# Gated attention on one core: where the output projection's sums of the first half are kept

## The chip, the core and the metric

The kernel runs on one core of a Trainium2 chip. Its engines work side by side, each through its own instructions in order: TensorE (PE in the profile, its weight loads PEld), VectorE (DVE), ScalarE (ACT), GpSimd (POOL) and SyncE (SP), which here only issues DMAs. GpSimd can issue DMAs too. The metric is the device time of one execution in microseconds (us).

## What is computed

One input x (2048 rows, 640 columns) is normalised row by row. From it come an attention over cached keys and values (32 heads of 128, the last 512 cached positions) with an output projection, and a gate from a two-layer network. Everything is float32.

```
xn = layernorm(x)
q  = xn @ wq                                  # per head: 2048 x 128
p  = softmax(q @ k.T * 128**-0.5)             # 512 cached positions
s  = sum over heads of (p @ v) @ wo[head]     # 2048 x 640
h  = relu(xn @ w1 + b1)**2
g  = silu(h @ w2 + b2)
out = x + s * g
```

The change concerns how the sum over heads in s is kept for the first half of the rows.

## The kernel before

**Products.** Each float32 factor is split into a high and a low part (tiles that end in 0 and 1 or hi and lo), and a product is three matmuls (`triple`). A column tile holds NT = 512 rows of x. There are four such tiles t; the first two are half 0 (hf = 0), the others half 1.

**Units.** The network of the gate runs first, for three of the four tiles. Then attention runs in 128 units. A unit is one head on one tile. In a half, heads go in 16 groups g of G = 2; a group runs tile 0 with both heads, then tile 1 with both heads: four units. A unit is spread over about three periods of PERIOD = 12.4 us of the plan, so that in each period TensorE works on parts of several units.

**The order.** Every step is put into a list with a time by `at` and `on`; the list is sorted by that time and each step is written out, so the time fixes only the order on each engine. `Ordered` keeps that order. Within a period, after the s matmuls (scores, in PSUM), VectorE folds the maxima (rdm), ScalarE gathers them, VectorE writes a row of them (rowm), SyncE sends it to DRAM (m_d) and reads it back broadcast to all partitions (bm, `row`). Then `shift` subtracts it on VectorE, e<-s,bm, which frees the s banks for the s matmuls of the next unit. ScalarE takes the exponential (e<-e) and the high part (pt_0_0, pt_1_0), and GpSimd the low parts (pt_0_1, pt_1_1) and the sum su. The o matmuls of the next period use pt. The raw weights come 10 us ahead of use and are split by ScalarE and GpSimd (wq, wk, wv, wo).

**The sums.** After the second head of a tile, `r_mm` multiplies both heads' outputs ot with wo, in five chunks d of 128 output columns, each into one PSUM bank r_d. `r_acc` empties it. In the first group (g = 0) ScalarE copies the bank into the tile acc (128 x 5 x 512); in the fifteen others VectorE adds the bank to acc in place. There are two acc tiles, one for each tile of the half (tag acc, bufs=TPH=2). After the last group of half 0, SyncE stores each chunk to s_d in DRAM (L591), ten stores of 256 KB, and the two tiles are taken over by half 1. `load_finish` and `finish` read s_d back later, during half 1, and form the output.

The five chunks are emptied at these places of the plan, counted from the start of the unit of the second head: d = 0 just past the start of the third period after it, d = 1 within that period, and d = 3, 2 and 4 in the fourth.

## Time and profile before

| | us |
|---|---|
| median of 3 runs | 1992.19 (1991.41 to 1992.53) |
| the profiled execution | 1990.35 |
| its span, first to last instruction | 1988.6 |
| plain part of the first half, 395 to 1034 | 49.2 per group of four units |
| additions acc<-r,acc on VectorE, both halves | 300, 662 ns each |
| copies acc<-r on ScalarE, first groups of both halves | 20, 577 ns each |
| stores s_d<-acc on SyncE's queue | 10, 256 KB each, 3.3 to landing |

A row of a timeline gives the start in us, the duration, the engine, the line (L72 is the helper that keeps the order, and so stands for nearly all of attention), the operation, out<-in, the count, and in brackets how long the engine had been idle and whom it waited for. A row of a window gives its length, each engine's busy time with its instructions, TensorE's granted clock, the busy share of the DMA engines and GB/s. A row of a group gives the count, the busy time in us, the mean in ns, and the idle time ahead.

### The profile page before, as it was taken

The page shows a single profiled execution, that of the slowest core. Times are in us where ns is not written, and L with a number is a line of the kernel's source. Part 1 is how long each engine was busy: PE and PEld are TensorE (multiplying, and loading weights), DVE is VectorE, ACT ScalarE, POOL GpSimd, SP SyncE. Part 2 cuts the span into 40 slices and gives each one's busy share as a digit, 9 for nine tenths or more (in the row PEclk, how much of TensorE's full clock was granted, in tenths as well). Part 3 has the DMA queues.
Part 4 walks back from the last instruction along what each step waited for, and adds up shares of the span by engine and source line. Part 5 has one row for each costly group of instructions (what it writes and reads, how often), then busy time and mean ns, then how long its engine had stood idle before and what let it go on. Part 6 is the DMA issues. An engine that isn't in the chain of part 4 may idle for free.

```text
span 1988.6 us, 25917 instructions
## 1 busy us (share of the span) xinstructions
PE 1958.7 (98%) x8576; PEld 1603.1 (81%) x8576; DVE 1515.5 (76%) x2511; ACT 1186.3 (60%) x2034; POOL 1375.3 (69%) x755
## 2 busy tenths in 40 slices
PE   7999999999999999999999999999999999999998
PEld 6788887788888888888887788888888888888877
DVE  5523236788888888888888878888888888888864
ACT  4432326766666666666666676666666666666643
POOL 1121225888888888888887788888888888888841
PEclk9999999999999999999999999999999999999999
DMA  4421444322323233222335433333333333333354
GB/s 137 136 106 38 180 171 144 105 91 94 95 93 91 91 91 91 91 90 92 94 93 170 157 98 107 112 112 113 112 112 115 113 112 113 96 91 91 110 147 141
DMA packets 126871, 220.39 MB, mean 111 GB/s; under 512 B 21542, under 2 KB 36304, under 8 KB 125456
## 3 DMA queue, kind: packets, MB, share of 16 engines
q1 hardware_dynamic: 123744, 204.28, 32.9%
q0 software_dynamic: 2992, 14.43, 1.8%
q8 instruction: 69, 1.13, 0.2%
q14 instruction: 66, 0.54, 0.1%
HBM read 194.26 MB, written 24.39 MB: 110 GB/s over the span
## 4 chain that ended last, share of the span: by engine, by line
PE 88%; DMA 4%; DVE 4%; ACT 2%; issue 1%; POOL 1%; SPq 0%; POOLq 0%; DVEq 0%; ACTq 0%
PE pq L72 20%; PE r L72 20%; PE o L72 17%; PE s L72 17%; PE py L96 2%; PE py L97 2%; PE py L95 2%; PE ph L97 2%; PE ph L96 2%; PE ph L95 2%; PE ly L72 2%; PE lu L72 1%; DMA w1r<-in_w_dram 1%; DMA bm<-m_d 1%; DVE rdm L72 1%
## 5 line engine op out<-in xcount | busy, mean ns | idle before, releaser
L72 POOL TENSOR_TENSOR pt<-e,pt 128x1024 fp32r<-128x1024 f32 x256 | 616.2, 2407 | 120.4 <-ACT pt L72 120.4
L72 PE MATMUL r<-ot,wo 128*128 128x512 f32 x1920 | 496.9, 389 | 0.2 <-DVE acc L72 0.2
L72 PE MATMUL pq<-ax,wq 128*128 128x512 f32 x1920 | 456.6, 389 | 0.8 <-DMA ax<-xT_d 0.7
L72 PEld LDWEIGHTS pq<-ax,wq 128*128 128x128 f32 x1920 | 360.6, 188 | 76.3 <-DMA ax<-xT_d 1.5
L72 PEld LDWEIGHTS r<-ot,wo 128*128 128x128 f32 x1920 | 360.3, 188 | 75.6 <-DVE acc L72 0.6
L72 PE MATMUL s<-q,wk 128*128 128x512 f32 x1536 | 372.1, 391 | 5.9 <-DVE e L72 5.9
L72 PE MATMUL o<-pt,wv 128*128 128x512 f32 x1536 | 374.6, 392 | 1.4 <-DVE ot L72 1.2
L72 ACT ACTIVATE e<-e 128x1024 f32<-128x1024 f32 x256 | 269.9, 1054 | 126.0 <-DVE e L72 122.1
L72 PEld LDWEIGHTS s<-q,wk 128*128 128x128 f32 x1536 | 287.9, 188 | 70.7 <-issue 7.2
L72 PEld LDWEIGHTS o<-pt,wv 128*128 128x128 f32 x1536 | 283.5, 188 | 72.9 <-DVE ot L72 14.9
L72 DVE TRANSPOSE_TENSOR_REDUCE rdm<-s 128x16 f32<-128x512 f32 (+1 forms) x384 | 313.4, 868 | 36.9 <-PE s L72 36.2
L72 DVE TENSOR_TENSOR e<-s,bm 128x512 f32<-128x512 f32 (+1 forms) x384 | 304.3, 842 | 17.0 <-DMA bm<-m_d 16.8
L72 POOL TENSOR_TENSOR su<-e,e 128x1024 f32<-128x1024 f32 x128 | 307.6, 2403 | 0.0
L72 ACT ACTIVATE pt<-e 128x1024 fp32r<-128x1024 f32 x256 | 272.0, 1062 | 7.9
L237 POOL TENSOR_TENSOR r<-r 128x512 f32<-128x512 f32 (+1 forms) x42 | 44.1, 1051 | 227.9 <-ACT r L278 208.8
L72 DVE TENSOR_TENSOR acc<-r,acc 128x512 f32<-128x512 f32 x300 | 198.6, 662 | 2.7 <-PE r L72 2.7
L72 ACT ACTIVATE ot<-o 128x512 fp32r<-128x512 f32 x128 | 76.8, 600 | 197.1 <-DVE o L72 197.1
L72 ACT ACTIVATE rds<-rds 32x32 f32<-32x32 f32 x384 | 87.7, 228 | 128.5 <-DVE rds L72 125.5
L72 DVE TRANSPOSE_TENSOR_REDUCE rds<-su 128x32 f32<-128x1024 f32 x128 | 158.1, 1235 | 0.1
L72 DVE TENSOR_TENSOR ot<-o,ot 128x512 fp32r<-128x512 f32 x128 | 88.6, 692 | 85.2 <-ACT ot L72 85.2
L72 POOL TENSOR_TENSOR wv<-vr,wv 128x512 fp32r<-128x512 f32 x64 | 83.2, 1300 | 81.5 <-ACT wv L72 74.4
L72 POOL TENSOR_TENSOR wq<-qr,wq 128x640 fp32r<-128x640 f32 x62 | 97.7, 1576 | 60.2 <-ACT wq L72 60.2
(123 smaller groups left out, 2168.6 us busy)
## 6 DMA issues: line engine op xcount, KB each, us to landing
bm<-m_d SPq DMA_DIRECT2D x128, 256.0 KB, 3.2
bs<-s_d SPq DMA_DIRECT2D x128, 256.0 KB, 3.8
qr<-in_wq_dram SPq DMA_DIRECT2D x64, 320.0 KB, 4.1
or<-in_wo_dram SPq DMA_DIRECT2D x64, 320.0 KB, 4.1
kr<-in_kT_dram SPq DMA_DIRECT2D x64, 256.0 KB, 3.4
vr<-in_v_dram SPq DMA_DIRECT2D x64, 256.0 KB, 4.3
xT_d<-xT POOLq DMA_DIRECT2D x6, 1280.0 KB, 7.5
xb<-in_x_dram SPq DMA_DIRECT2D x16, 320.0 KB, 3.4
```

The source lines that it names most:

```text
L72: ins = method(*args, **kwargs)
L95: nc.tensor.matmul(ps, ah, bh, start=first and i == 0, stop=False)
L96: nc.tensor.matmul(ps, ah, bl, start=False, stop=False)
L97: nc.tensor.matmul(ps, al, bh, start=False, stop=last and i == n - 1)
L237: nc.gpsimd.tensor_tensor(r, r, r, op=ALU.mult)
```

## The change

In half 0 every group is now treated like the first: ScalarE copies each bank into an acc tile, which is a new one for each tile and group (the same two buffers in turn). After the fifth chunk, a new step `r_store` sends the whole tile, 1280 KB, to s_d from GpSimd's queue with one DMA. In group 0 that DMA writes; in the others it adds to what is in DRAM (accum_op), with the five chunks of a partition as five pieces. SyncE's ten stores are gone. Half 1 is as before.

```diff
     def r_acc(i, d):
         hf, g, t, h = units[i]
         pr = PRS.pop((i, d))
+        if d == 0 and (hf == 0 or g == 0):
+            ACC[hf, t] = keep.tile(
+                [P, DC, NT], F32, tag="acc", name=f"acc{hf}_{t}_{g}", bufs=TPH
+            )
+        a = ACC[hf, t][:, d, :]
+        if hf == 0 or g == 0:
+            act.activation(a, pr, AF.Copy)
+        else:
+            dve.tensor_tensor(a, pr, a, op=ALU.add)
+
+    def r_store(i):
+        hf, g, t, h = units[i]
         if g == 0:
-            if d == 0:
-                ACC[hf, t] = keep.tile(
-                    [P, DC, NT], F32, tag="acc", name=f"acc{hf}_{t}", bufs=TPH
-                )
-            act.activation(ACC[hf, t][:, d, :], pr, AF.Copy)
+            pool.dma_start(s_d[t], ACC[hf, t])
         else:
-            a = ACC[hf, t][:, d, :]
-            dve.tensor_tensor(a, pr, a, op=ALU.add)
-        if g == NG - 1 and hf == 0:
-            sp.dma_start(s_d[t][:, d, :], ACC[hf, t][:, d, :])
+            pool.dma_start(s_d[t], ACC[hf, t], accum_op=ALU.add, max_dma_last_dim=4 * NT)
...
                     on(when + 0.68 * len(js), r_acc, i, d)
+                if d == DC - 1 and hf == 0:
+                    on(4 * PERIOD + 9.2, r_store, i)
```

ScalarE's order in one odd period of the second group, before (e is the exponential, rdm the gather of maxima, rds that of sums, ot and q high parts, wv and wq weights):

```order
L72 ACTIVATE e_0_3440<-e_0_3440 128x1024 [waits DVE_49,Pool_49]
L72 ACTIVATE pt_0_0_3465<-e_0_3440 128x1024 [waits Activation_49]
L72 ACTIVATE e_1_3449<-e_1_3449 128x1024 [waits DVE_49,Pool_49]
L72 ACTIVATE pt_1_0_3484<-e_1_3449 128x1024 [waits PE_49,Activation_49]
L72 ACTIVATE rdm_3476<-rdm_3476 32x64 [waits DVE_49]
L72 ACTIVATE rdm_3476<-rdm_3476 32x64 x2
L72 ACTIVATE ot_3515<-o_3426 128x512 [waits DVE_49]
L72 ACTIVATE q_0_3527<-pq_3495 128x512 [waits PE_49]
L72 ACTIVATE rds_3524<-rds_3524 32x32 [waits DVE_49]
L72 ACTIVATE rds_3524<-rds_3524 32x32 x2
L72 ACTIVATE wv_5_0_3542<-vr_5_3442 128x512 [waits DMAHW0_49]
L72 ACTIVATE wq_6_0_3546<-qr_6_3444 128x640 [waits DMAHW1_49]
```

The same place now:

```order
L72 ACTIVATE acc_0_1_3338<-r_3_3454 128x512 [waits PE_49]
L72 ACTIVATE pt_0_0_3468<-e_0_3443 128x1024 [waits Activation_49]
L72 ACTIVATE e_1_3452<-e_1_3452 128x1024 [waits DVE_49,Pool_49]
L72 ACTIVATE pt_1_0_3487<-e_1_3452 128x1024 [waits Activation_49]
L72 ACTIVATE rdm_3479<-rdm_3479 32x64 [waits DVE_49]
L72 ACTIVATE rdm_3479<-rdm_3479 32x64 x2
L72 ACTIVATE acc_0_1_3338<-r_2_3406 128x512 [waits PE_49]
L72 ACTIVATE ot_3518<-o_3429 128x512 [waits DVE_49]
L72 ACTIVATE q_0_3530<-pq_3498 128x512 [waits PE_49]
L72 ACTIVATE rds_3527<-rds_3527 32x32 [waits DVE_49]
L72 ACTIVATE rds_3527<-rds_3527 32x32 x2
L72 ACTIVATE acc_0_1_3338<-r_4_3533 128x512 [waits PE_49]
```

Three copies have come in: ahead of pt_0_0, ahead of ot, and behind rds, where the weight splits wv and wq follow as before. In an even period there are two, of r_0 ahead of pt_0_0 and of r_1 ahead of ot. The copy of r_0 is the first into its tile and waits for the store that last read that buffer:

```order
L72 ACTIVATE acc_1_1_3596<-r_0_3583 128x512 [waits DMASW4_49,PE_49]
L72 ACTIVATE pt_0_0_3598<-e_0_3572 128x1024 [waits Activation_49]
L72 ACTIVATE e_1_3581<-e_1_3581 128x1024 [waits DVE_49,Pool_49]
L72 ACTIVATE pt_1_0_3617<-e_1_3581 128x1024 [waits Activation_49]
L72 ACTIVATE rdm_3609<-rdm_3609 32x64 [waits DVE_49]
```

These rows follow two weight splits behind the ones above, in the next even period, and belong to tile 1. DMASW is a count that a DMA of GpSimd's queue raises when it has landed.

GpSimd's order at the end of the same odd period and in the even one behind it, before (su is the sum of e):

```order
L72 TENSOR_TENSOR wv_5_1_3543<-vr_5_3442,wv_5_0_3542 128x512 [waits DMAHW0_49,PE_49,Activation_49]
L72 TENSOR_TENSOR wq_6_1_3547<-qr_6_3444,wq_6_0_3546 128x640 [waits DMAHW1_49,Activation_49]
L72 TENSOR_TENSOR pt_0_1_3594<-e_0_3568,pt_0_0_3593 128x1024 [waits Activation_49,Pool_49]
L72 TENSOR_TENSOR su_3626<-e_0_3568,e_1_3577 128x1024 [waits Activation_49]
L72 TENSOR_TENSOR pt_1_1_3613<-e_1_3577,pt_1_0_3612 128x1024 [waits Activation_49]
```

And now:

```order
L72 TENSOR_TENSOR wv_5_1_3546<-vr_5_3445,wv_5_0_3545 128x512 [waits DMAHW0_49,PE_49,Activation_49]
L72 TENSOR_TENSOR wq_6_1_3550<-qr_6_3447,wq_6_0_3549 128x640 [waits DMAHW1_49,Activation_49]
L72 DMA s_d_77<-acc_0_1_3338 128x5x512 [waits DMASW5_49,DMASW3_49]
L72 TENSOR_TENSOR pt_0_1_3599<-e_0_3572,pt_0_0_3598 128x1024 [waits Activation_49,Pool_49]
L72 TENSOR_TENSOR su_3631<-e_0_3572,e_1_3581 128x1024 [waits Activation_49]
L72 TENSOR_TENSOR pt_1_1_3618<-e_1_3581,pt_1_0_3617 128x1024 [waits PE_49,Activation_49]
```

The store has come in between the weight splits and the three long instructions on e. It waits for the store before it into the same sum.

## The prediction

> **What bounds the kernel now.** I read the busy times first, then a table of stages by windows, then one pair of periods of the first half instruction by instruction. A period starts with the s matmuls of one unit. Even periods hold the sums of r_0 and r_1 of a group, odd ones those of r_3, r_2 and r_4.

> ```profile
> PE 1958.7 (98%) x8576; PEld 1603.1 (81%) x8576; DVE 1515.5 (76%) x2511; ACT 1186.3 (60%) x2034; POOL 1375.3 (69%) x755
> core 0: us, PE busy (x) PEld busy (x) DVE busy (x) ACT busy (x) POOL busy (x), PEclk, DMA share, GB/s
> 641.00:690.20 49.20, 49.20 (x219) 40.49 (x218) 42.15 (x71) 32.33 (x57) 39.96 (x21) 1.00 0.29 92
> ...
> 1034.60:1084.00 49.40, 48.61 (x213) 39.41 (x212) 41.24 (x70) 31.82 (x56) 38.80 (x21) 1.00 0.50 155
> 1084.00:1133.00 49.00, 47.07 (x206) 37.92 (x204) 39.79 (x66) 30.26 (x51) 38.83 (x20) 1.00 0.49 162
> 1133.00:1182.00 49.00, 48.57 (x214) 39.91 (x213) 38.05 (x64) 34.75 (x63) 38.92 (x21) 1.00 0.35 113
> ```

> TensorE is busy in all 49.20 us of a group of four units, at full clock. Work taken from VectorE there has no gap of TensorE to fill. The only losses near the change lie at the turn between the halves: 0.79, 1.93 and 0.43 us, 3.15 in all. So the question is not what the change frees but which of TensorE's just-in-time inputs it makes late. Two matter: the row of maxima that goes out to DRAM and comes back broadcast (m_d, then bm) before VectorE can subtract it and free the s bank, and GpSimd's low parts pt before the o matmuls.

> ```profile
> 659.07 0.32 SPq L72 DMA_DIRECT2D m_d<-rowm  x1
> 659.96 2.41 POOL L72 TENSOR_TENSOR pt<-e,pt 128x1024 fp32r<-128x1024 f32 x1
> 660.42 0.33 SPq L72 DMA_DIRECT2D bm<-m_d  x1
> 661.70 2.93 PE L72 MATMUL o<-pt,wv 128*128 128x512 f32 x12
> 664.22 2.37 DVE L72 TENSOR_TENSOR e<-s,bm 128x1024 f32<-128x1024 f32 x3
> 665.83 2.88 PE L72 MATMUL s<-q,wk 128*128 128x512 f32 x12
> ...
> 671.36 0.33 SPq L72 DMA_DIRECT2D m_d<-rowm  x1
> 676.22 2.37 DVE L72 TENSOR_TENSOR e<-s,bm 128x1024 f32<-128x1024 f32 x3
> 677.15 1.59 POOL L72 TENSOR_TENSOR wq<-qr,wq 128x640 fp32r<-128x640 f32 x1
> 678.07 2.88 PE L72 MATMUL s<-q,wk 128*128 128x512 f32 x12
> 679.78 2.41 POOL L72 TENSOR_TENSOR pt<-e,pt 128x1024 fp32r<-128x1024 f32 x1 [1.04 <-ACT pt L72]
> ```
> ```profile
> bm<-m_d SPq DMA_DIRECT2D x128, 256.0 KB, 3.2
> L72 DVE TENSOR_TENSOR e<-s,bm 128x1024 f32<-128x1024 f32 x128 | 151.3, 1182 | 17.0 <-DMA bm<-m_d 16.8
> ```

> In the even period bm is issued at 660.42 and lands 3.2 us later, at 663.6. The next s matmuls start at 665.83 and need the first subtraction, 1.18 us, so it may start at 664.65: **bm has 1.0 us to spare**. The odd period has less, as a late one shows:

> ```profile
> 695.90 0.33 SPq L72 DMA_DIRECT2D m_d<-rowm  x1
> 698.14 0.33 SPq L72 DMA_DIRECT2D bm<-m_d  x1
> 701.46 2.42 DVE L72 TENSOR_TENSOR e<-s,bm 128x1024 f32<-128x1024 f32 x3 [0.64 <-DMA bm<-m_d]
> 702.83 1.39 PE L72 MATMUL s<-q,wk 128*128 128x512 f32 x5
> ```

> Here m_d took 2.24 us where it mostly takes 1.35 (660.42 less 659.07). VectorE waited 0.64, the subtraction ended at 702.64, and the s matmuls at 702.83 just held.

> **The change, part by part.** Removed are 150 additions on VectorE, added 150 copies on ScalarE:

> ```profile
> L72 DVE TENSOR_TENSOR acc<-r,acc 128x512 f32<-128x512 f32 x300 | 198.6, 662 | 2.7 <-PE r L72 2.7
> L72 ACT ACTIVATE acc<-r 128x512 f32<-128x512 f32 x20 | 11.5, 577 | 0.0
> ```

> VectorE loses 150 x 0.662 = 99 us of work. That is worth nothing, since TensorE is full and covers it. ScalarE gains 150 x 0.577 = 87 us; per group 32.3 + 10 x 0.577 = 38.1 of 49.2, which fits. What counts is what a copy delays behind it in ScalarE's order. One stands between e and pt in every period. The first group of the half already has its copies on ScalarE, so this is in the trace:

> ```profile
> 382.38 1.06 ACT L72 ACTIVATE e<-e 128x1024 f32<-128x1024 f32 x1 [0.25 <-DVE e L72]
> 383.35 0.58 ACT L72 ACTIVATE acc<-r 128x512 f32<-128x512 f32 x1
> 383.83 1.05 ACT L72 ACTIVATE pt<-e 128x1024 fp32r<-128x1024 f32 x1
> ...
> 652.96 1.06 ACT L72 ACTIVATE e<-e 128x1024 f32<-128x1024 f32 x1 [1.02 <-DVE e L72]
> 654.05 1.06 ACT L72 ACTIVATE pt<-e 128x1024 fp32r<-128x1024 f32 x1
> 657.58 0.79 ACT L72 ACTIVATE rdm<-rdm 32x64 f32<-32x64 f32 x3 [0.42 <-DVE rdm L72]
> 669.87 0.79 ACT L72 ACTIVATE rdm<-rdm 32x64 f32<-32x64 f32 x3 [0.18 <-DVE rdm L72]
> ```

> From e to pt it is 1.45 us with the copy and 1.09 without: 0.36 us later. The gather rdm, which starts the way to m_d, had waited 0.42 us for VectorE in the even period, which hides it; in the odd period 0.18 of it is hidden and m_d goes out 0.18 us later. That eats into the margin of late odd periods like that of 695.90. The queue's timeline has about ten of them in the first half, one in six periods; at some 0.15 us each **1.5 us**. The copies of r_1 and r_2 fall into the wait of ot for VectorE. That of r_4 delays the two weight splits behind it by about 0.75 us, with the 0.18; they are not due for a period.

> The ten stores of s_d on SyncE's queue at the turn go. They cost SyncE about 0.4 us each and TensorE at most part of the 3.15 us, so I take nothing.

> New are 32 stores of 1280 KB on GpSimd's queue, 30 of them adding. They stand behind the weight splits of an odd period and ahead of the three long instructions pt, su, pt. Each waits for the last copy and for the store before it into the same sum (one group, 49 us, earlier). Queued behind it are those three, and the o matmuls wait for them. First its issue:

> ```profile
> L72 POOL DMA_DIRECT2D xT_d<-xT x16 | 8.9, 557 | 0.0
> L303 POOL DMA_DIRECT2D br<-in_b_dram x3 | 1.7, 578 | 0.2 <-issue 0.2
> ```

> The weight split that ended at 677.15 + 1.59 = 678.74 now ends 0.75 later, 679.5; pt's input comes 0.36 later, at 680.14. So 0.64 us are free. Behind them the second pt may slip: in the even period shown it ended at 659.96 + 2.41 = 662.37, while the eighth of twelve o matmuls, the first to use it, comes at 661.70 + 7 x 0.24 = 663.4. Of that 1.0 us the copy takes 0.36. An issue up to 0.64 + 0.65 = **1.3 us** costs nothing. The rows show 0.56 us for 128 rows and 0.58 for a few, so no growth with rows; but no row has five pieces per partition. Bounds: 0.56, and five times as much, 2.8. I take the lower, which both rows support: **0**.

> Then its transfer. Below stand two issues in order of time, their time to landing (the DMA view of 120 to 135 us), the time to landing of all such loads (the page), and the busy tenths of the DMA engines from 681 to 692 us in slices of 0.275 us:

> ```profile
> 123.58 1.06 POOL L72 DMA_DIRECT2D xT_d<-xT  x2
> 124.43 1.26 SPq L144 DMA_DIRECT2D xb<-in_x_dram  x2
> ...
> xT_d<-xT POOLq DMA_DIRECT2D x2, 1280.0 KB, 8.0
> xb<-in_x_dram SPq DMA_DIRECT2D x2, 320.0 KB, 8.9
> ...
> xb<-in_x_dram SPq DMA_DIRECT2D x16, 320.0 KB, 3.4
> ...
> DMA  9997100000000000014555410000000000001456
> ```

> The first pair of rows is two plain 1280 KB stores from GpSimd's queue and two loads on SyncE's queue 0.85 us later. The stores landed 8.0 us after issue, and the loads took 8.9 us instead of 3.4. So a store on one queue does hold up a load on the other, by up to 5.5 us for 256 rows. The last row shows the stretch that an adding store will fall into: the DMA engines stand idle there from 682.4 until bm's data runs, from slice 17 (685.7) to 23 (687.3).

> An adding store must read the old sum as well as the tile. Its length is not in the trace: the lower bound is half the pair, 4 us, and the upper has none but the design's (24 us, below). I take the whole pair, 8 us, for twice the bytes. Issued at about 680.0, it lands at 688: m_d and the whole of bm's data lie inside it, once per store. The cost to bm's 128 rows lies between 0 and 128/256 x 5.5 = 2.75 us. I take half, 1.4, because the engines are only half busy while bm runs. The 16 rows of m_d add 16/256 x 5.5 = 0.34. Less the margin: 1.4 + 0.34 - 1.0 = 0.74 us of TensorE, 30 times, **22 us**. The odd period's bm runs some 17 us after the issue and is clear.

> [...]

> Sum: 1990.35 (the profiled execution) + 22 + 1.5 = 2014. The median of before lies 1.84 above that execution, so I forecast **2016 us**.

> **The rivals.** *Drained in time: no change.* If the store lands within 5.7 us of its issue (680.0 to 685.7), bm meets nothing. Only the 1.5 us stay: 1992 by the profiled execution, 1994 by the median. For it: idle DMA engines, and 1.0 us of slack that forgives a short overlap. Against it: the pair's 8.0.

> *Strict turns.* Each row of bm waits as long as xb's did: 2.75 + 0.34 - 1.0 = 2.1 us, 30 times, 63 us: 2055, 2057 by the median. [...] Against it: bm's rows are a fifth as long as those stores' rows, and so are the new pieces.

> *Issue bound.* If five pieces per partition cost 2.8 us to issue, GpSimd is 1.5 us late for the o matmuls, 30 times, 45 us: 2039 by the median. A stall there also gives bm the same time, so the larger of the two counts, not both. It decides from 1.3 us. Against it: the flat rows.

> *The copy waits.* Each staging tile is written again two periods after its store: 49.2 / 2 less 0.6, 24 us. A store slower than that blocks ScalarE, whose order holds everything else. At 30 us it is 6 x 30 = 180 us: some 2170.

> *Faster.* All that could be won is the 3.15 us at the turn, which is under 0.2%, about what a measurement of this kernel can tell from no change.

> **How the numbers follow.** Forecast 0.36 (its own range 1998 to 2036), drained in time 0.32, strict turns 0.12, issue bound 0.12, the copy waits 0.05, faster by something I do not see 0.03. So faster 0.03, same 0.32, slower 0.65. The range takes in the first four, from 1989 to 2057, and leaves out the last two.

> **What would show it.** Right: in the first half windows of about 50.7 instead of 49.20 us with TensorE idle some 0.7 us ahead of s once in two periods, released by VectorE's e, which waits for bm; bm's time to landing in even periods over 4 us, in odd ones 3.2; the new store landing in about 8 us; its issue near 0.6. Wrong: s without gaps and bm at 3.2 (drained); gaps ahead of o released by GpSimd's pt and an issue over 1.3 us (issue bound); ScalarE's acc waiting for the store (the copy waits). A store landing far beyond 8 us would also reach the odd periods' bm, with less margin, and break the sum upward.

## The result, and the profile after

The changed kernel takes **2130.35 us** (median of four runs, 2120.53 to 2138.62), the one before 1991.8 beside it (median of four, 1990.9 to 1992.53): a ratio of 1.069, with a 95% interval of 1.064 to 1.074. It is slower, as forecast, but by 139 us where 24 were forecast, and the time lies outside the range. The four runs of the changed kernel go with the clock that TensorE was granted: 0.981 in the one of 2120.53, 0.974 in the one of 2138.62. The profiled execution of the changed kernel spans 2118.7 us, 130.1 more than the 1988.6 of before.

First the busy times, the chain of work that ended last (shares of the span) and four groups of the changed kernel. A group's columns are count | busy us, mean ns | idle us ahead of it, and what ended it; the last row is a DMA with its size and its time to landing.

```profile
PE 2000.7 (94%) x8576; PEld 1625.4 (77%) x8576; DVE 1436.4 (68%) x2361; ACT 1250.6 (59%) x2184; POOL 1418.0 (67%) x787
PE 68%; DMA 16%; DVE 9%; ACT 4%; issue 1%; POOL 0%; SPq 0%; ACTq 0%; DVEq 0%; POOLq 0%
L72 PE MATMUL s<-q,wk 128*128 128x512 f32 x1536 | 403.6, 415 | 90.8 <-DVE e L72 90.6
L72 DVE TENSOR_TENSOR e<-s,bm 128x512 f32<-128x512 f32 (+1 forms) x384 | 306.1, 849 | 127.2 <-DMA bm<-m_d 126.5
L72 ACT ACTIVATE acc<-r 128x512 f32<-128x512 f32 x170 | 98.0, 576 | 6.5 <-PE r L72 6.4
L72 POOL DMA_DIRECT2D s_d<-acc x32 | 46.0, 1438 | 0.0
s_d<-acc POOLq DMA_DIRECT2D x32, 1280.0 KB, 11.5
```

For comparison, the chain and one group of the kernel before:

```profile
PE 88%; DMA 4%; DVE 4%; ACT 2%; issue 1%; POOL 1%; SPq 0%; POOLq 0%; DVEq 0%; ACTq 0%
L72 PE MATMUL s<-q,wk 128*128 128x512 f32 x1536 | 372.1, 391 | 5.9 <-DVE e L72 5.9
```

The reader is to see two things. TensorE's pauses ahead of s grew from 5.9 to 90.6 us: **84.7**. And TensorE's own busy time grew with the same number of matmuls, from 1958.7 to 2000.7: **42.0**, of which s has 31.5 (403.6 less 372.1; 415 ns each instead of 391). Together that is 126.7 of 130.1. The chain's share of DMA went from 4 to 16%.

Where the pauses come from shows in one even period and the odd one behind it, from the timeline of the changed kernel (start, duration, engine, operation, and in brackets the idle time ahead and whom it waited for):

```profile
695.71 1.51 POOL L72 DMA_DIRECT2D s_d<-acc  x1
696.64 3.02 POOL L72 TENSOR_TENSOR pt<-e,pt 128x1024 fp32r<-128x1024 f32 x1
700.02 0.32 SPq L72 DMA_DIRECT2D m_d<-rowm  x1
705.29 0.33 SPq L72 DMA_DIRECT2D bm<-m_d  x1
708.87 2.42 DVE L72 TENSOR_TENSOR e<-s,bm 128x1024 f32<-128x1024 f32 x3 [4.03 <-DMA bm<-m_d]
710.24 4.58 PE L72 MATMUL s<-q,wk 128*128 128x512 f32 x12 [3.03 <-DVE e L72]
...
717.10 0.32 SPq L72 DMA_DIRECT2D m_d<-rowm  x1
718.44 0.33 SPq L72 DMA_DIRECT2D bm<-m_d  x1
721.67 2.37 DVE L72 TENSOR_TENSOR e<-s,bm 128x1024 f32<-128x1024 f32 x3
724.19 2.88 PE L72 MATMUL s<-q,wk 128*128 128x512 f32 x12
...
739.59 3.00 PE L72 MATMUL s<-q,wk 128*128 128x512 f32 x12 [3.00 <-DVE e L72]
```

The store is issued at 695.71. The row of maxima m_d, 2 KB, goes out 4.3 us later and takes 5.27 us (705.29 less 700.02); in the odd period it takes 1.34. The broadcast bm, 256 KB, then needs 3.55 us, hardly more than its 3.2 of before, as the chain of waits gives it (start, length):

```profile
700.02 5.25 DMA m_d<-rowm
705.29 3.55 DMA bm<-m_d
```

So it is the tiny transfer that is held, and bm, which cannot start without it, is late by as much.

The second thing is the clock. Windows of the same execution (length, busy us with instructions of PE, PEld, DVE, ACT and POOL, then TensorE's granted clock, DMA share, GB/s):

```profile
710.24:767.35 57.11, 51.45 (x217) 41.37 (x217) 36.94 (x61) 36.55 (x67) 42.65 (x22) 0.97 0.55 125
705.00:710.20 5.20, 2.21 (x10) 1.47 (x8) 1.33 (x2) 0.32 (x2) 2.57 (x2) 1.00 0.44 101
710.20:714.80 4.60, 4.56 (x13) 3.64 (x14) 3.06 (x4) 4.48 (x5) 1.99 (x1) 0.63 0.69 186
739.50:744.50 5.00, 4.91 (x22) 4.08 (x23) 3.58 (x5) 4.90 (x7) 2.33 (x1) 1.00 0.48 168
```

The first row is one group, from the s of one even period to that of the next but one. It takes 57.1 us instead of 49.2: TensorE is idle for 5.7 of them, and its other 51.5 hold what filled 49.2 before. For behind the pause that ended at 710.24 the granted clock is 0.63, so that twelve s matmuls take 4.58 us instead of 2.9; behind the equal pause that ended at 739.59 it stays at 1.00. Over the whole execution the granted clock is 0.981, before 0.999. What is missing to 1, times the span, is 40.3 us now and 2.0 before, so the clock accounts for 38 of the 42.0 us; the other 4 stay open.

### The profile page after: what moved, and what is told of

The parts are those of the page before. It is cut to its first block, busy times and chain, and to the rows that moved or that the text cites. A ratio compares the mean times of both kernels' runs of the same rounds, so it can differ in the third digit from the quotient of the medians.

```text
span 2118.7 us, 25916 instructions
## 1 busy us (share of the span) xinstructions
PE 2000.7 (94%) x8576; PEld 1625.4 (77%) x8576; DVE 1436.4 (68%) x2361; ACT 1250.6 (59%) x2184; POOL 1418.0 (67%) x787
## 3 DMA queue, kind: packets, MB, share of 16 engines
q0 software_dynamic: 22960, 56.37, 13.0%
## 4 chain that ended last, share of the span: by engine, by line
PE 68%; DMA 16%; DVE 9%; ACT 4%; issue 1%; POOL 0%; SPq 0%; ACTq 0%; DVEq 0%; POOLq 0%
PE s L72 14%; PE r L72 13%; PE pq L72 13%; PE o L72 11%; DMA m_d<-rowm 8%; DMA bm<-m_d 6%; DVE rdm L72 4%; DVE e L72 3%; PE ph L96 2%; PE py L96 2%; PE ph L95 2%; PE py L97 2%; PE ph L97 2%; PE py L95 2%; PE ly L72 2%; ACT rdm L72 2%
## 5 line engine op out<-in xcount | busy, mean ns | idle before, releaser
L72 POOL TENSOR_TENSOR pt<-e,pt 128x1024 fp32r<-128x1024 f32 x256 | 639.6, 2498 | 211.2 <-ACT pt L72 210.9
L72 PE MATMUL r<-ot,wo 128*128 128x512 f32 x1920 | 500.3, 391 | 0.2 <-DVE acc L72 0.2
L72 PE MATMUL s<-q,wk 128*128 128x512 f32 x1536 | 403.6, 415 | 90.8 <-DVE e L72 90.6
L72 PE MATMUL pq<-ax,wq 128*128 128x512 f32 x1920 | 456.8, 389 | 3.3 <-DMA ax<-xT_d 3.3
L72 PEld LDWEIGHTS s<-q,wk 128*128 128x128 f32 x1536 | 306.3, 202 | 171.1 <-issue 103.2
L72 PEld LDWEIGHTS r<-ot,wo 128*128 128x128 f32 x1920 | 363.2, 189 | 77.6 <-DVE acc L72 0.7
L72 PEld LDWEIGHTS pq<-ax,wq 128*128 128x128 f32 x1920 | 360.4, 188 | 79.2 <-DMA ax<-xT_d 4.0
L72 ACT ACTIVATE e<-e 128x1024 f32<-128x1024 f32 x256 | 269.9, 1054 | 217.5 <-DVE e L72 214.4
L72 DVE TENSOR_TENSOR e<-s,bm 128x512 f32<-128x512 f32 (+1 forms) x384 | 306.1, 849 | 127.2 <-DMA bm<-m_d 126.5
L72 DVE TRANSPOSE_TENSOR_REDUCE rdm<-s 128x16 f32<-128x512 f32 (+1 forms) x384 | 316.0, 869 | 102.7 <-PE s L72 102.1
L72 PE MATMUL o<-pt,wv 128*128 128x512 f32 x1536 | 377.8, 393 | 4.2 <-POOL pt L72 2.5
L72 PEld LDWEIGHTS o<-pt,wv 128*128 128x128 f32 x1536 | 284.3, 188 | 78.1 <-POOL pt L72 11.7
L72 POOL TENSOR_TENSOR su<-e,e 128x1024 f32<-128x1024 f32 x128 | 319.5, 2496 | 0.0
L72 ACT ACTIVATE pt<-e 128x1024 fp32r<-128x1024 f32 x256 | 271.0, 1059 | 5.9
L72 ACT ACTIVATE ot<-o 128x512 fp32r<-128x512 f32 x128 | 76.7, 599 | 150.9 <-DVE o L72 150.9
L72 DVE TRANSPOSE_TENSOR_REDUCE rds<-su 128x32 f32<-128x1024 f32 x128 | 158.1, 1235 | 3.3 <-POOL su L72 3.1
L72 ACT ACTIVATE rds<-rds 32x32 f32<-32x32 f32 x384 | 87.5, 228 | 112.8 <-DVE rds L72 109.8
L72 DVE TENSOR_TENSOR ot<-o,ot 128x512 fp32r<-128x512 f32 x128 | 88.5, 692 | 85.2 <-ACT ot L72 85.2
L72 POOL TENSOR_TENSOR wv<-vr,wv 128x512 fp32r<-128x512 f32 x64 | 83.0, 1296 | 77.6 <-ACT wv L72 70.5
L72 POOL TENSOR_TENSOR wq<-qr,wq 128x640 fp32r<-128x640 f32 x62 | 97.6, 1574 | 46.9 <-ACT wq L72 46.9
L72 ACT ACTIVATE rdm<-rdm 32x64 f32<-32x64 f32 x384 | 97.8, 255 | 50.5 <-DVE rdm L72 46.2
## 6 DMA issues: line engine op xcount, KB each, us to landing
s_d<-acc POOLq DMA_DIRECT2D x32, 1280.0 KB, 11.5
bm<-m_d SPq DMA_DIRECT2D x128, 256.0 KB, 3.3
bs<-s_d SPq DMA_DIRECT2D x128, 256.0 KB, 3.6
kr<-in_kT_dram SPq DMA_DIRECT2D x64, 256.0 KB, 4.0
vr<-in_v_dram SPq DMA_DIRECT2D x64, 256.0 KB, 4.2
xT_d<-xT POOLq DMA_DIRECT2D x6, 1280.0 KB, 7.5
```

The lines of the kernel that those rows point to most:

```text
L72: ins = method(*args, **kwargs)
```

## The experiments

Two questions: what in the change holds m_d, and whether the lower clock comes from the pauses or from the traffic. My theory was that the bytes of a long transfer on GpSimd's queue hold whatever comes later on SyncE's. Its rivals were ScalarE's new order, the issue on GpSimd, the adding, the direction of the transfer, and the weight loads on SyncE's own queue. Each run is one execution, so a difference of a few us between two of them says nothing; the kernel before ran on the same chips at 1990.12 (copies alone, plain stores in one piece, adding store later, store in two parts), 1988.38 (plain stores in five pieces, bm without m_d, load, few bytes), 1990.57 (three chunks, pause without a store) and 1992.15 (the two with the weight loads moved).

**The copies alone.** The adding stores are left out, so the sums of groups 1 to 15 are missing from the output.

```diff
         if g == 0:
             pool.dma_start(s_d[t], ACC[hf, t])
-        else:
-            pool.dma_start(s_d[t], ACC[hf, t], accum_op=ALU.add, max_dma_last_dim=4 * NT)
```

> Leaves out the 30 adding stores: the sum in DRAM holds the first group alone; the 150 copies on ScalarE stay. Held write (the store in flight holds the row of maxima on its way to DRAM): with no store there is nothing to hold it, m_d back at 1.34 us, 1990 to 1996 us. ScalarE's order (the copies make the maxima or pt late): nothing of its cause is gone, about 2130 us. GpSimd (the issue of 1.49 us and the slower pt and su behind it): its cause is gone too, so as held write.

Measured: 1996.62, pauses of s 13.9 us, PE busy 1957.9. So ScalarE's order is not the cause. Most of the 6.5 us over the kernel before comes from the two plain stores of the first group, which stayed. The first of them, in the timeline:

```profile
385.13 0.56 POOL L72 DMA_DIRECT2D s_d<-acc  x1
389.46 0.32 SPq L72 DMA_DIRECT2D m_d<-rowm  x1
394.78 0.33 SPq L72 DMA_DIRECT2D bm<-m_d  x1
399.16 3.00 PE L72 MATMUL s<-q,wk 128*128 128x512 f32 x12 [2.82 <-DVE e L72]
```

Beside a plain store m_d takes 5.3 us here, with an issue of 0.56: neither adding nor a long issue is needed. The second pause is 2.33 us; the two make 5.2, and 1.3 of the 6.5 are left for the 150 copies. Away from these two and from the turn between the halves, s pauses twice in the first half, by 1.57 and 0.71 us, where m_d took 3.4 and 3.1; that the copies are the reason there is not shown.

**Plain stores.** As changed, but each store overwrites instead of adding (so only the last group's sum remains), first in one piece per partition, then in the five pieces of the change.

```diff
-            pool.dma_start(s_d[t], ACC[hf, t], accum_op=ALU.add, max_dma_last_dim=4 * NT)
+            pool.dma_start(s_d[t], ACC[hf, t])                              # first run
+            pool.dma_start(s_d[t], ACC[hf, t], max_dma_last_dim=4 * NT)     # second run
```

> Leaves out the addition: each of the 32 stores writes its tile over the last one's, at the same place, with the same bytes from SBUF, in one piece per partition. Held write, if any 1280 KB store holds m_d while it runs: it should land after some 5 us, about when m_d goes out (4.1 to 5.2 us behind it), so m_d at 1.4 to 2.5 us, inside the 1.0 us to spare or little over, 1992 to 2020 us. If the length of the adding store is what counts, near 1994. ScalarE's order: about 2130. GpSimd: an issue of 0.56 us instead of 1.49, 1992 to 1996.

> Leaves out the addition, but keeps the five pieces per partition: 32 plain stores, each over the last one's tile. If the pieces make the issue long, it stays near 1.5 us, if the adding does, it is 0.56. If the adding (a second read) makes the store long, it lands after about 7 us as in the plain store of one piece, m_d comes back after 2 to 4.5 us and the time is 2035 to 2060; if the pieces do, it lands after about 11.5, m_d takes 4.9 and the time is 2120 to 2140.

Measured: 2046.76 and 2050.59. The stores land in 7.2 and 7.6 us, are issued in 0.58 and 0.86, and s pauses for 42.3 and 47.0 us. The first lies above all that I had expected, because the store landed after 7.2 us and not 5; the second lies in the first of its cases. So not quite half of the loss is there without adding. The adding store is longer, 11.5 against 7.6 with the same pieces asked for, and its issue 1.44 against 0.86. The queue did not send the same pieces, though: for the same 56.37 MB the page counts 22960 packets of GpSimd's queue in the changed kernel and 13360 here.

**The adding store later**, behind GpSimd's second pt of the even period, where m_d and bm have passed.

```diff
-                    on(4 * PERIOD + 9.2, r_store, i)
+                    on(4 * PERIOD + 19.0, r_store, i)
```

> The same adding stores, but written out behind the second pt of the even period instead of ahead of the first, some 8 us later, so that the even period's m_d is away before the store starts. Held write: m_d of even periods back at 1.34; that of the odd period, 9 us behind the issue, falls into the last 1 to 3 us of the store and comes back up to 2 us late against 0.7 to spare, so stalls of 0 to 1.5 us: 1995 to 2040 us. ScalarE's order: about 2130. GpSimd: the issue now stands ahead of the weight splits with slack behind it, 1992 to 2000.

Measured: 2080.86, above what I expected. The pauses of s shrink to 20.1 us, but o now waits 57.4 us for ot. The timeline shows the other row, that of the sums (rows, then bs), in the place of m_d:

```profile
661.49 0.33 SPq L72 DMA_DIRECT2D bm<-m_d  x1
663.59 1.47 POOL L72 DMA_DIRECT2D s_d<-acc  x1
664.81 0.32 SPq L72 DMA_DIRECT2D s_d<-rows  x1
668.11 0.32 SPq L72 DMA_DIRECT2D bs<-s_d  x1
674.74 0.70 DVE L72 TENSOR_TENSOR o<-o,bs 128x512 f32<-128x512 f32 x1 [2.37 <-DMA bs<-s_d]
676.85 3.06 PE L72 MATMUL o<-pt,wv 128*128 128x512 f32 x12 [1.66 <-DVE ot L72]
```

bm lands as before, but the 2 KB of rows take 3.3 us instead of 1.3, and the 256 KB of bs 6.6 instead of 3.8. This place is one of the few in which rows is held: in 22 of the 30 it is issued 1.0 us behind the adding store, ahead of the store's data, and takes 1.3; bs then takes 8.4 (median), and m_d of the odd period, 8.4 us behind the store, 5.0. I had overlooked that SyncE's queue carries two such round trips in each period, so that a store of this length has no free place.

**The store in two parts**, two chunks behind the pt of one period and three behind that of the next.

```diff
-                    on(4 * PERIOD + 9.2, r_store, i)
+                    on(3 * PERIOD + 19.0, r_store, i, 0)     # chunks 0 and 1, 512 KB
+                    on(4 * PERIOD + 19.0, r_store, i, 1)     # chunks 2 to 4, 768 KB
```

> The sum complete, but each store cut in two: chunks 0 and 1 behind the second pt of the odd period, chunks 2 to 4 behind that of the next even one, so that each part runs between the return of one period's maxima and the departure of the next's (about 7.7 us). Held write: parts of some 5 and 7 us fit, m_d at 1.34 in nearly all periods, 1990 to 2000 us. ScalarE's order: about 2130. GpSimd: 64 issues of 0.7 to 1.0 us, but at a place with slack, 1992 to 2005.

Measured: 2055.11, a miss for the same reason: s waits 29.7 us for e, in 19 places, and o 26.0 us for ot, in 31.

**bm without m_d.** As changed, but bm reads the maxima of the unit before, whose row has long been in DRAM. The exponentials then subtract another unit's maxima, which the division by their sum takes out again.

```diff
+        if what == "m":
+            MD.append(d)
+            d = MD[-2:][0]
         bc = ap.tile([P, NT], F32, tag=f"b{what}", name=f"b{what}{i}", bufs=2)
```

> bm is read from the row of maxima of the unit before, which has long landed, so bm no longer waits for m_d (the softmax is then shifted by another unit's maxima). All stores as in the change. If only the small write m_d is held, bm goes out right behind m_d and lands after 3.3 us in time: the s matmuls do not wait, 1995 to 2015 us. If the store holds whatever SyncE's queue sends while it runs, reads as well, bm itself takes 6 to 7 us, 1 to 2 us over what there is to spare: 2030 to 2075 us. ScalarE's order or GpSimd as cause: unchanged near 2130.

Measured: 2053.59, as expected of a hold on everything that SyncE's queue sends.

```profile
668.74 1.49 POOL L72 DMA_DIRECT2D s_d<-acc  x1
672.86 0.33 SPq L72 DMA_DIRECT2D m_d<-rowm  x1
673.24 0.42 SPq L72 DMA_DIRECT2D bm<-m_d  x1
680.46 2.42 DVE L72 TENSOR_TENSOR e<-s,bm 128x1024 f32<-128x1024 f32 x3 [2.61 <-DMA bm<-m_d]
```

bm, issued 0.38 us behind m_d, still takes 7.2 us instead of 3.2. As medians of this run, the 256 KB of bm take 6.8 and the 2 KB of m_d 5.0, so each is held by 3.6: the hold does not go with the size of what is held. Half the pauses are gone (46.1 us), because bm no longer waits for m_d: from m_d's issue to bm's landing it is 7.1 us now (median), 8.3 in the changed kernel.

**A load in place of the store**: GpSimd reads as many bytes back from s_d into the tile (no sum is added).

```diff
-            pool.dma_start(s_d[t], ACC[hf, t], accum_op=ALU.add, max_dma_last_dim=4 * NT)
+            pool.dma_start(ACC[hf, t], s_d[t], max_dma_last_dim=4 * NT)
```

> Leaves out the addition and the storing: the 30 adding stores become plain loads of the same 1280 KB in five pieces per partition, from s_d into the tile, at the same place on GpSimd's queue. If what holds m_d is the store's traffic of writes to DRAM, m_d is back at 1.34 and the time near 1996 to 2005. If it is that a long transfer of one queue is far ahead on the DMA engines when the small one comes, in whichever direction, m_d takes 2 to 4.5 us as with the plain store, 2030 to 2060.

Measured: 2071.85, above the 2060 that I allowed for; the loads land in 8.2 us and s pauses for 61.3 us. So a load holds m_d too, and it is not the writing that does.

**Few bytes, the same pieces**: adding, 640 pieces, each a sixteenth as long (80 KB in all; the other columns are left out of the sums).

```diff
-            pool.dma_start(s_d[t], ACC[hf, t], accum_op=ALU.add, max_dma_last_dim=4 * NT)
+            n = NT // 16
+            pool.dma_start(s_d[t][:, :, :n], ACC[hf, t][:, :, :n], accum_op=ALU.add)
```

> Leaves out fifteen sixteenths of each addition: the adding stores keep their 640 pieces, but each is 32 columns of a chunk instead of 512, 80 KB in all. GpSimd's issue stays near 1.5 us if the number of pieces makes it. Held write: the store is over before m_d goes out, m_d 1.34, 1996 to 2003 us. GpSimd (long issue as the cause): o waits for pt, at most 0.2 us more often than now, and the time stays above 2050.

Measured: 2002.63, with the first group's two plain stores still in it (s pauses 13.0 us in all).

```profile
L72 POOL DMA_DIRECT2D s_d<-acc x32 | 41.9, 1308 | 0.0
s_d<-acc POOLq DMA_DIRECT2D x30, 80.0 KB, 5.1
```

The issue is nearly as long as in the change, yet m_d, issued 4.4 us behind it, takes 1.34. So the issue on GpSimd does not hold m_d. Although the transfer lands only after 5.1 us, its data are nearly through by then: in 17 of the 30 places all 640 packets had begun before m_d was issued, in ten at most 120 had not. In the other three, at the turn between the halves, 457 to 635 were still to come, and m_d took 3.1 to 4.8 us although the bytes are few (other transfers run there as well). So what holds m_d is packets in front of it, and not that the transfer has still to land.

**Three chunks of five**, 768 KB instead of 1280.

```diff
-            pool.dma_start(s_d[t], ACC[hf, t], accum_op=ALU.add, max_dma_last_dim=4 * NT)
+            pool.dma_start(s_d[t][:, 2:], ACC[hf, t][:, 2:], accum_op=ALU.add, max_dma_last_dim=4 * NT)
```

> The changed kernel, but from the second group on only chunks 2 to 4 are added (768 KB; the sums of chunks 0 and 1 are left at the first group's). If a latecomer waits for what is left of the store: such a store is over 7 to 8 us after its issue, m_d comes 4.3 us after it and takes 2.3 to 3.5 us instead of 4.9, s waits 25 to 55 us in all, 2020 to 2060. If any store in flight holds a latecomer by the same 3.6 us: m_d 4.7 to 5.0, s waits 80 to 95 us, 2100 to 2135. If the price goes with the share of the bytes in flight, as the prediction had it: m_d 1.5 to 1.7, 1995 to 2005.

Measured: 2087.68, between my first two cases. These stores land in 9.2 us, later than I took them to, and m_d takes 4.38.

**The weight loads out of the way.** Ahead of m_d, SyncE's own queue carries two weight loads (at 695.04 and 695.80 in the period shown above). A store that slows them could hold m_d behind them on its own queue. So both are issued behind bm in the 32 periods concerned, once in the changed kernel and once in the kernel before.

```diff
-                    at(base + when - 10.5, load_raw, kind, hf, h)
+                    u = round((base + when - 8.4) / PERIOD)
+                    late = 6.4 if u % 2 == 0 and 6 <= u <= 68 else 0.0
+                    at(base + when - 10.5 + late, load_raw, kind, hf, h)
```

> The changed kernel with every store as it is; in the 32 even periods with a store the two raw weight loads (576 or 640 KB), which SyncE issues just ahead of m_d, are issued behind bm instead. If m_d waits for the store itself: m_d near the stores stays at 4.4 to 5.4 us, s waits 75 us or more, 2090 us or more. If m_d waits on its own queue behind the weight loads, which the store has slowed: m_d near the stores 1.3 to 2.0 us, s waits under 45 us, and the time under 2070; what is left then comes from bm beside the store and from the splits that wait for the later loads.

> The kernel before with the same loads moved behind bm in the same 32 periods, for the price of the move alone: the weight splits of ScalarE and GpSimd come up to 2 us later and hold the exponential behind them by up to 1 us; 1990 to 2030 us, m_d 1.33 in all periods. By the theory that m_d waits behind loads on its own queue, m_d in even periods does not change here, because without a store the loads have landed when it comes.

Measured: 2146.18 and 2009.50. In the changed kernel with the loads moved:

```profile
644.57 0.32 SPq L72 DMA_DIRECT2D bs<-s_d  x1
...
646.38 1.49 POOL L72 DMA_DIRECT2D s_d<-acc  x1
651.56 0.32 SPq L72 DMA_DIRECT2D m_d<-rowm  x1
656.11 0.32 SPq L72 DMA_DIRECT2D bm<-m_d  x1
```

The first of the moved loads follows at 656.47. Nothing is left ahead of m_d on its queue but bs, seven us old, and m_d still takes 4.55 us. It waits for the store, not for the loads. In the kernel before the same move leaves m_d at 1.33 and costs 17 us by itself.

**A pause without a store**, for the clock: the kernel before, where in the same 32 periods the row of maxima makes two more small hops before bm reads it.

```diff
         sp.dma_start(d, r)
+        if what == "m" and i % 2 == 0 and 6 <= i <= 68:
+            r = ap.tile([B32, B32], F32, tag="hop", name=f"hop{i}", bufs=2)[:NQ]
+            sp.dma_start(r, d)
+            d = dpool.tile([NQ, B32], F32, tag="h2_d", name=f"h2_d{i}", bufs=4)
+            sp.dma_start(d, r)
```

> The kernel before, without any store from GpSimd; in the 32 even periods in which the change has a store in flight, the row of maxima takes two more small hops (DRAM to SBUF and back) before bm reads it, so that bm is late by some 3 to 4 us with nothing else on the queues. If the lower granted clock of the changed kernel comes from TensorE's pauses of about 3 us alone: pauses of s of 70 to 100 us in all, and on top of that PE busy 1985 to 2005 us and granted clock near 0.98, 2090 to 2135 us in all. If it comes from the traffic beside the matmuls: PE busy stays at 1956 to 1964 us with clock 0.999, and the time is that of before plus the pauses alone, 2060 to 2090.

Measured: 2080.41. By the time alone this lies in the range of the second theory, because the pauses are a little shorter than either assumed; the busy time and the clock, 0.987, are as the first has it.

```profile
PE 1987.1 (96%) x8576; PEld 1616.5 (78%) x8576; DVE 1521.9 (73%) x2511; ACT 1184.4 (57%) x2034; POOL 1372.2 (66%) x755
L72 PE MATMUL s<-q,wk 128*128 128x512 f32 x1536 | 394.7, 408 | 68.2 <-DVE e L72 68.1
638.00:643.00 5.00, 4.99 (x15) 3.99 (x16) 3.83 (x6) 4.07 (x4) 2.76 (x2) 0.66 0.50 163
```

Without any transfer of GpSimd, 62 us more pauses bring 28.4 us more busy time of TensorE, 0.46 per us of pause; the change has 42.0 for 84.7, which is 0.50. The clock itself accounts for 25 of the 28.4 (27.0 us missing to full clock, less 2.0). So the lower clock is the pauses' own price, and traffic is not needed for it.

**Together.** The runs line up by what was left of the transfer when m_d was issued. "Lands in" is the median over all of a run's transfers, "m_d issued after" (the transfer's issue) and "m_d takes" are medians over the 24 to 28 even periods of the first half with a transfer issued 3 to 7 us before m_d; "left" is the time to landing less that distance.

| kernel | lands in | m_d issued after | left | m_d takes | s idle ahead, in all |
|---|---|---|---|---|---|
| 80 KB, adding | 5.1 | 4.4 | 0.7 (few packets) | 1.34 | 13.0 |
| plain, one piece | 7.2 | 4.2 | 3.0 | 3.27 | 42.3 |
| plain, five pieces | 7.6 | 4.2 | 3.4 | 3.38 | 47.0 |
| load, five pieces | 8.2 | 4.2 | 4.0 | 3.93 | 61.3 |
| adding, 768 KB | 9.2 | 4.2 | 5.0 | 4.38 | 74.0 |
| adding, loads moved | 10.0 | 4.8 | 5.2 | 4.63 | 98.7 |
| the change | 11.5 | 4.6 | 6.9 | 4.87 | 90.8 |

Up to about 5 us, m_d lands about when the transfer does; beyond that it levels off, because m_d gets in before the transfer is over. The trace of the changed kernel shows it in the period above. These are packets, MB and share of 16 engines' time by queue (q0 is GpSimd's, q1 SyncE's), first from m_d's issue, 700.02, to 703.60, then from there to its landing, 705.29:

```profile
q0 software_dynamic: 333, 0.68, 106.4%
q1 hardware_dynamic: 2, 0.00, 0.1%
```
```profile
q0 software_dynamic: 170, 0.35, 111.7%
q1 hardware_dynamic: 30, 0.00, 2.8%
```

For 3.6 us hardly anything but the store runs; then m_d's packets pass (16 of 128 B, 16 of 4 B), with the store's running beside them, and some 90 of the store's 640 still follow. The medians over the 30 adding stores say the same: m_d's first packet comes 3.6 us after its issue, behind 351 packets of the store, and behind m_d's last one 117 are still to come. With the loads moved it is 3.6 us, 361 and 39; with bm freed from m_d 3.6 us, 349 and 147. So in these runs the latecomer waited for the rest of the transfer or, behind an adding store that had more left, for about 22 of its 2 KB packets for each of the 16 DMA engines (351 by 16, if they are spread evenly). What sets the 22 no run shows.

No variant with the sums complete came nearer to the kernel before than the 2055.11 of the store in two parts, and with TensorE full in the first half there was little to win for one.

## Why the prediction was wrong, point by point

*TensorE is full, so relief of VectorE is worth nothing.* Right. VectorE's busy time fell by 79 us (1515.5 to 1436.4), and with the copies alone the time did not fall.

*The copies cost 1.5 us.* The size fits, 1.3 being left in the run with the copies alone, but that is within what single runs differ by, and the ten pauses of 0.15 were not seen: there were two, of 2.3 us together. *The copy waits*, a rival, is out: ScalarE's acc waited 6.5 us in all, 6.4 of them for TensorE.

*The issue takes 0.56 us and costs nothing.* The size was wrong, 1.44, and above the point of 1.3 at which I said it would decide. Still *issue bound* did not happen: TensorE waited 2.5 us in all for pt, since the pause of s comes first and gives GpSimd its time. An issue of 1.31 with no pause behind it (80 KB) cost o no more than 1.9 us.

*The store lands in 8 us.* It took 11.5. The guess of twice the bytes rested on the length of the plain pair, and its 8.0 was the middle of two that ran into each other, 6.35 and 9.75; a plain store of this form alone takes 7.2 to 7.6, so the adding one lands half as late again. Some of the landing passes without data: the first packet runs 2.75 us after the issue (median). The packets' own time differs by more. On the pages, GpSimd's queue has 2.1% of 16 engines' span with the copies alone, 6.8% with plain stores in five pieces and 13.0% in the change, which is 3.2 us for each plain store and 7.8 for each adding one, 2.4 times as long at the same count of bytes (56.37 MB in both runs); whether the adding does it or the packets, half as large (2 KB instead of 4), was not separated.

*m_d 0.34 us, by its share of rows.* **This is the step that failed.** I scaled the hold of xb (5.5 us for 256 rows) with the number of rows of what is held, and so gave m_d's 16 rows next to nothing. Measured, m_d is held by 3.5 us (4.87 less 1.33), ten times as much; the weight loads do not cause it, and bm's 128 rows, when they come at the same moment, are held by 3.6, no more than m_d beside them. What counted here was how much of the store passed first, not what was held. The trace behind the row of xb shows both parts: the first packet of the loads comes 3.0 us after the issue at 124.43, behind packets of GpSimd's queue, and only then do the two queues share, 154 of the 256 packets of the loads among 157 of the stores. I took the whole 5.5 us for the second part, and let it grow with the rows, which was my estimate; the first was paid by m_d's 16 rows as well, 3.5 us.

*bm 1.4 us.* It cost 0.3 in the changed kernel, since m_d had already waited out most of the store. *The margin of 1.0 us* fits, and the place was right: with the measured holds the term becomes 3.54 + 0.3 - 1.0 = 2.84 us, 30 times, 85 us, against 84.7 measured. That the direction came out is owed to the place, and not to how the price was split: bm's was 1.1 us too high and m_d's 3.2 too low. *The odd periods are clear*: right, m_d 1.34 there.

*Strict turns*, the rival nearest to what happened, fell short, at 2057, for the same reason: it scaled with rows as well. (*The copy waits*, at 2170, has the nearer number and did not happen.) In the traces m_d's few rows wait behind some 351 of the adding store's packets (3.6 us), or for the rest of the store where that is shorter, as in the upper rows of the table; by what rule the queues follow each other was not shown.

*A term that was not there at all* is the added busy time of TensorE, 42.0 us, of which the clock accounts for 38. A stall of TensorE was priced at its length; here each us of it cost about another half.

So the sum, by its own steps: 1990.35 + 84.7 (pauses of s) + 42.0 (busy time, mostly the clock) + 3.4 (the rest) = 2120.5, the profiled execution; the median lies 9.8 above that. Of the signs to look for, the place of the pauses and their releaser were as written; the length of a group (57 instead of 50.7), the store (11.5 instead of 8), its issue (1.44 instead of 0.6) and bm (3.5, not over 4) were not.

## What to carry to other kernels

Before a long transfer is put beside a chain of small ones that an engine waits for, find those that are issued while its data run (here from some 2.7 us after its issue), and charge each with the rest of the transfer, however small it is, up to a limit, which was 3.6 us here; count every round trip of the queue in a period, since moving the transfer past one puts it ahead of the next. And where TensorE is full, charge a stall with its length and with a third to a half again for the clock that can follow (0.50 in the change, 0.46 without traffic, 0.32 with the store later).

## What the runs showed of the hardware that was not expected

- **The clock fell after some pauses and not after others, and the length of a pause alone did not tell which.** Two s blocks of the run with pauses alone:

```profile
424.98 3.00 PE L72 MATMUL s<-q,wk 128*128 128x512 f32 x12 [3.12 <-DVE e L72]
773.23 4.18 PE L72 MATMUL s<-q,wk 128*128 128x512 f32 x12 [1.83 <-DVE e L72]
```

  So in these traces a window need not be idle throughout: 1.94 us of its 3.41, little more than half, were enough in every case.
- **The adding DMA in 640 pieces was long even with few bytes**: 80 KB took 5.1 us to land, and 1.31 to issue. No plain one in the same pieces was run.
- **GpSimd computed more slowly behind an adding store.** In the timeline of the changed kernel pt takes 3.02 us there and 2.4 elsewhere. With plain stores the mean of all pt stays as before, with the change it rises:

```profile
L72 POOL TENSOR_TENSOR pt<-e,pt 128x1024 fp32r<-128x1024 f32 x256 | 616.0, 2406 | 167.8 <-ACT pt L72 166.5
L72 POOL TENSOR_TENSOR pt<-e,pt 128x1024 fp32r<-128x1024 f32 x256 | 639.6, 2498 | 211.2 <-ACT pt L72 210.9
```

  The first row is the run with plain stores in one piece, the second the change. It cost little here: TensorE waited 2.5 us in all for pt. Why it happens was not tried.
